# Four layer-norms on GpSimd, two constants first on VectorE, the last stores on two DMA queues, and a new list of pieces

## The chip, the cores and the metric

The kernel runs on one core of one Trainium2 chip. A core has a matrix engine (TensorE, PE in the profile; its weight loads are PEld), three engines that work on rows of 128 partitions (VectorE, DVE; ScalarE, ACT; GpSimd, POOL) and SyncE (SP), which does nothing but issue DMA transfers. Each engine has its own stream of instructions and goes through it in order; semaphores tie the streams together. The metric is the time of one execution on the device, in microseconds (us); lower is better.

## The reference

One activation `x` of 2,048 tokens by 512 is normalized once and goes through two branches whose results are added to it: an attention with a memory that is carried over four segments of 512 tokens (32 heads of 16), and a dense layer with SiLU (512 to 1,792 to 512). All tensors are bf16.

```
xn = _layernorm(x, axis=-1)
return x + _A_ref(xn, A_wq, A_wk, A_wv, A_wo, A_beta) + _B_ref(xn, B_w1, B_w2)

# _A_ref, for each segment s of 4, L = 512
logits = jnp.einsum('bhqd,bhkd->bhqk', qs, ks) * scale + mask
p = _softmax(logits, axis=-1)
a_dot = jnp.einsum('bhqk,bhkd->bhqd', p, vs)
pq = phi(qs)
num = jnp.einsum('bhld,bhde->bhle', pq, M)
den = jnp.einsum('bhld,bhd->bhl', pq, z)[..., None] + 1e-06
o = g * (num / den) + (1.0 - g) * a_dot
pk = phi(ks)
M = M + jnp.einsum('bhld,bhle->bhde', pk, vs)
z = z + jnp.einsum('bhld->bhd', pk)
# after the segments: o @ wo

# _B_ref
out = jnp.einsum('bsf,fd->bsd', _silu(jnp.einsum('bsd,df->bsf', x, w1)), w2)
```

`phi(t)` is `t + 1` where `t > 0` and `exp(t)` elsewhere, `g` is the sigmoid of `A_beta` for each head.

## The kernel before

The tokens are 16 tiles of 128 (`x` tile `t`), four to a segment. For each segment `s` the kernel makes `k`, `q` (features on partitions, four blocks `dt` of 128 features, 8 heads each), `v` (tokens on partitions), the dense layer's hidden values `h` (14 blocks), the attention, and the output product, which adds 14 products of the dense layer and 4 of the attention into one bank of PSUM per tile.

The softmax of a segment and a `dt` is cut into five blocks, `S` number `20 s + 5 dt + b`. A block's scores fill `psS`, four banks of PSUM, of which there is one; one ScalarE instruction of 128 x 2,048 exponentiates them into a buffer `Pb` (seven of them), and GpSimd zeroes the upper triangle in the diagonal blocks (`scores`, L653 to L682; one mask instruction, or two where `b` is 1 or 4). Heads of odd number read `kTo`, a copy of `kT` with the even heads zeroed, which GpSimd makes behind each copy of `k` (L362). When the five blocks of a `dt` are there, `E` multiplies the weights with `v` for the even heads (blocks 0, 1, 2) and `O` for the odd ones (blocks 3, 1, 4); `V` carries ones beside the values, so each product brings its sums too. The copies out of PSUM (`Ev`, `Ov` on VectorE, `Ea`, `Oa` on ScalarE) are followed by moves on the SP queue: two that gather the sums into `zraw` (L711), and behind an odd copy four more that put the odd heads' rows into `oraw` (L730).

A segment's sums become reciprocals (`r`, or `R` for the last segment, where they come in two parts: the first three `dt`, then the fourth), are multiplied by the gate (`w`, `W`) and spread over partitions by two SP moves each (`z` for the attention's weights, `d` for the memory's; L542). Then `dv` scales the features, `n` multiplies them with the memory on TensorE, `zv` scales the attention's output, and `nv` adds the two into `oT`. The last output products of a tile read `oT` (pieces `o s.j.14` to `o s.j.17`, one for each `dt`; pieces `oc` and `od` are a half and a quarter of one, `oh` is half of the last tile's width, `st` and `sh` add `x` and store).

Nothing in the source's order of functions sets the order of work. A text, `ORDER` (L16), names every piece of work once, and the kernel issues the pieces in that order (L786 on); so the text fixes each engine's stream, and each queue's. The first letters say what a piece is and on which engine it runs: `k0.2.1` is a part of the product for `k` of segment 0, block 2; `kv` and `ka` are its copy on VectorE and ScalarE; `ha` is the tanh of the dense layer on ScalarE and `hv` its product on VectorE; `xs` are a tile's statistics on VectorE, `xg4.4` the inverse roots of tiles 4 to 7 on GpSimd, `Nv` a norm on VectorE and `Na` on GpSimd, `XD` the transpose of a normalized tile by DMA (SP); `fp`, `fa`, `fv` and `gp`, `ga`, `gv` are the parts of phi of `k` and `q` on GpSimd, ScalarE and VectorE; `t`, `m`, `mv` the memory's product; `xl` loads a tile of `x` again for the final sum; `lw` loads weights. Each line of `ORDER` after the first begins with an `S`, so a line is what is issued between two blocks of scores.

Between blocks of scores TensorE works on four groups of columns of 32 (lines L324, L696 of the profile, form 128*32) or on the whole array (L322); scores work on groups of rows (L662).

Before the list, outside it, the loads of `x` and the weights are issued, `zraw` is zeroed on VectorE, `ident` and `b16` are made on GpSimd. `make_odd` reads `b16` and makes `pm_odd`, which `kTo` needs; `make_kind` reads `ident` and makes four small vectors that the sums of segment 0 are the first to need.

Of the kernel before, what the change touches and what calls it, by code (L numbers as in the profile page):

```python
# [16 lines left out]
ones0 ones1 zeros xc0 xd0 xc1 xq0 xi0 Nv0 busy44 xd1 xq1 xc2 xi1 X0.1 Nv1 xd2 Xa0.1 busy6 v0.0.0 v0.0.1 xq2 X1.1 Xa1.1 xs3 v0.0.2 v0.0.3 xq3 v0.1.0 xi2 v0.1.1 v0.1.2 v0.1.3 odd Nv2 xi3 X2.1 va0.0 k0.2.0 va0.1 Nv3 Xv2.1 X3.1 Xv3.1 k0.0.0 k0.0.1 k0.0.2 k0.0.3 q0.0.0 kv0.0 tb q0.0.1 q0.0.2 xs4 q0.0.3 qa0.0 k0.2.1 q0.3.0 fa0.0 q0.1.0  # L17
S1 k0.2.2 xs6 q0.1.1 v0.3.0 v0.3.1 xs7 q0.3.1 q0.1.2 q0.1.3 xs5 xg4.4 q0.3.2 qa0.1 q0.3.3 fp0.0
S2 k0.2.3 v0.3.2 qv0.3 v0.3.3 k0.1.0 kv0.2 fp0.2 fa0.2 k0.1.1 vv0.3 k0.1.2 k0.1.3 q0.2.0 q0.2.1
S3 kv0.1 q0.2.2 h0.10.0 h0.10.1 Nv4 fv0.0 q0.2.3 h0.10.2 v0.2.0 h0.10.3 qv0.2 ha0.10 k0.3.0 k0.3.1  # L20
S0 Nv5 v0.2.1 k0.3.2 hv0.10 h0.11.0 k0.3.3 h0.11.1 h0.11.2 kv0.3 h0.11.3 Nv7 xs8 XD5 ha0.11 h0.7.0
S7 h0.7.1 h0.1.0 h0.7.2 h0.7.3 v0.2.2 h0.1.1 v0.2.3 XD4 h0.1.2 h0.1.3 hv0.11 Nv6 ha0.7
S6 h0.13.0 fp0.3 XD7 h0.13.1 vv0.2 hv0.7 E0 XD6 v1.1.0 h0.13.2 h0.13.3 ha0.1 v1.1.1 Ev0
S5 fv0.2 h0.5.0 v1.1.2 h0.5.1 hv0.1 v1.1.3 vv1.1 v1.3.0 h0.5.2 ha0.13 xs14 hv0.13 h0.5.3 ha0.5 t0.2 v1.3.1
S9 hv0.5 xs12 q1.1.0 v1.3.2 v1.3.3 fa0.3 q1.1.1 q1.1.2 E1 k1.1.0 q1.1.3
S4 qv1.1 k1.1.1 vv1.3 fv0.3 k1.0.0 k1.0.1 k1.0.2 lw0 h0.4.0 k1.1.2 Ev1 h0.4.1 k1.0.3 k1.1.3 kv1.1
S17 h0.8.0 h0.8.1 kv1.0 h0.4.2 O0 xs10 h0.4.3 h0.2.0 Ov0 ha0.4
S10 h0.2.1 k1.2.0 xs11 xs9 k1.2.1 h0.2.2 k1.2.2 h0.2.3 h0.8.2 ha0.2 t0.3 hv0.4 xg8.4 t0.0 k1.2.3
# [73 lines left out]
def kernel(  # L102
# [19 lines left out]
    NT = S // P  # L122
# [11 lines left out]
    out_flat = out.flatten_outer_dims()  # L134
# [40 lines left out]
    def load_w(eng, w_sb, W, k0, k1):  # L175
# [11 lines left out]
        out=beta_r[:], in_=bass.AP(tensor=A_beta.tensor, offset=A_beta.offset, ap=[[1, H], [0, 4], [1, 1]])  # L187
# [646 lines left out]
```

## Time and profile before

| what | value |
|---|---|
| median of 3 runs | 229.09 us (228.93 to 229.31) |
| the profiled execution, time | 229.25 us |
| its span | 227.4 us |
| granted TensorE clock | 1.00 |
| 80 exponentials (L669), busy on ScalarE | 150.2 us, 1.878 each |
| 56 tanh (L457), busy on ScalarE | 32.8 us |
| first and 80th exponential, start | 12.89 and 205.93 us |
| HBM | 9.96 MB read, 2.10 MB written, 53 GB/s over the span |

The profile is of one execution, with times from the start of its span. Busy time counts what an engine executes; "idle before" is the time an engine sat still ahead of an instruction, and behind the arrow stands what ended it. In a timeline a row is a run of like instructions, with start and length in us; an engine's name with a q is its sequencer (SPq issues DMAs). In busy time by stretch a row has the stretch, its length, the busy time and the number of instructions of PE, PEld, DVE, ACT and POOL, then the granted clock, the busy share of the DMA engines and GB/s.

### The profile page before, as it was taken

Reading aid. Unit: us, or ns where it says so; the run is one execution under the profiler, and the core shown is the slowest. Engines: PE = TensorE matmul, PEld = TensorE weight load, DVE = VectorE, ACT = ScalarE, POOL = GpSimd, SP = SyncE. Lnnn points to the kernel's source line nnn. Section 1 sums busy time; section 2 is a strip of 40 time slices with the busy share of each in tenths; the row PEclk is TensorE's granted clock in tenths of the full one; section 3 lists DMA queues with packets and bytes.
Section 4 is the critical chain, followed back from the end, with each engine's and each line's share of the span. In section 5 each row is a group of like instructions: output and inputs, shape, how many; then the busy total and the mean of one; then the engine's idle time right before and its main releaser. Section 6 shows DMA issues by size and latency. Waiting matters only on the chain.

```text
span 227.4 us, 7551 instructions
## 1 busy us (share of the span) xinstructions
PE 217.5 (96%) x3127; PEld 113.3 (50%) x3155; DVE 177.1 (78%) x350; ACT 198.5 (87%) x180; POOL 113.9 (50%) x173
## 2 busy tenths in 40 slices
PE   8999999999999999999999999999999999999993
PEld 8676645545444434444544444445444544445661
DVE  3799899987897797658798898846776987985834
ACT  3799998999999999999999899999999989897000
POOL 6049647767454673665544578545464364342000
PEclk9999999999999999999999999999999999999999
DMA  6991419323215213414123312141132212024032
GB/s 189 369 379 46 85 36 313 62 45 66 61 22 156 73 35 48 95 34 100 36 61 87 90 45 59 32 119 40 37 93 65 80 40 81 31 68 128 16 95 95
DMA packets 34787, 20.55 MB, mean 90 GB/s; under 512 B 15680, under 2 KB 34240, under 8 KB 34752
## 3 DMA queue, kind: packets, MB, share of 16 engines
q1 hardware_dynamic: 32128, 17.45, 28.0%
q10 hardware_dynamic: 2624, 2.62, 3.6%
q8 instruction: 24, 0.39, 0.7%
q14 instruction: 11, 0.09, 0.1%
HBM read 9.96 MB, written 2.10 MB: 53 GB/s over the span
## 4 chain that ended last, share of the span: by engine, by line
PE 67%; ACT 17%; DVE 7%; issue 4%; POOL 2%; DMA 1%; DVEq 0%; SPq 0%; ACTq 0%
PE ps L322 20%; PE psO L322 13%; ACT Pb L669 12%; PE psO L324 8%; PE psS L662 8%; PE ps L324 6%; PE psV L696 5%; PE psS L324 3%; ACT th L457 3%; PE psS L756 2%; ACT ex L395 1%; DVE hT L462 1%; DVE kT L361 1%; DVE qT L371 1%; DVE xn_t L301 1%
## 5 line engine op out<-in xcount | busy, mean ns | idle before, releaser
L669 ACT ACTIVATE Pb<-psS 128x2048 bf16<-128x2048 f32 x80 | 150.2, 1878 | 4.7 <-PE psS L662 4.0
L677 POOL TENSOR_SCALAR_AFFINE_SELECT Pb<-Pb 128x512 bf16<-128x512 bf16 (+1 forms) x112 | 79.1, 720 | 84.3 <-ACT Pb L669 83.0
L462 DVE SCALAR_TENSOR_TENSOR hT<-th,ps 128x512 bf16<-128x512 bf16 x56 | 37.7, 679 | 14.4 <-ACT th L457 13.7
L322 PE MATMUL ps<-xnT,w_sb 128*128 128x512 bf16 (+1 forms) x177 | 43.3, 340 | 0.8 <-issue 0.5
L322 PE MATMUL psO<-w_sb,hT 128*128 128x512 bf16 (+2 forms) x137 | 36.0, 339 | 0.7 <-issue 0.5
L457 ACT ACTIVATE th<-ps 128x512 bf16<-128x512 f32 x56 | 32.8, 598 | 0.6 <-PE ps L322 0.6
L324 PE MATMUL psO<-w_sb,hT 128*32 128x512 bf16 (+2 forms) x476 | 27.6, 301 | 0.0
L322 PEld LDWEIGHTS <-w_sb 128*128 128x128 bf16 x184 | 17.1, 98 | 16.3 <-issue 3.3
L696 PE MATMUL psV<-Pb,Vz 128*32 128x128 bf16 (+3 forms) x512 | 23.1, 300 | 0.2
L324 PE MATMUL ps<-xnT,w_sb 128*32 128x512 bf16 (+1 forms) x384 | 21.8, 329 | 0.0
L322 PEld LDWEIGHTS <-hT 128*128 128x128 bf16 x147 | 13.4, 98 | 16.6 <-issue 4.8
L324 PEld LDWEIGHTS <-hT 128*32 128x32 bf16 x644 | 15.9, 97 | 9.3 <-issue 1.7
L662 PE MATMUL psS<-qT,kT 16*128 16x128 bf16 (+3 forms) x256 | 17.3, 301 | 0.9 <-ACT Pb L669 0.8
L696 PEld LDWEIGHTS <-Vz 128*32 128x32 bf16 x512 | 13.1, 96 | 10.3 <-DVE hT L462 1.1
L662 PE MATMUL psS<-qT,kTo 32*128 32x384 bf16 (+3 forms) x256 | 17.2, 299 | 0.6 <-ACT Pb L669 0.2
L362 POOL TENSOR_SCALAR kTo<-kT,pm_odd 128x512 bf16<-128x512 bf16 x16 | 12.3, 771 | 8.4 <-DVE kT L361 7.5
L322 PE MATMUL ps<-xnT,wk_sb 128*128 128x512 bf16 (+1 forms) x66 | 15.4, 328 | 0.7 <-issue 0.5
L322 PE MATMUL ps<-wv_sb,xnT 128*128 128x512 bf16 x48 | 14.3, 380 | 0.6 <-DVE odd L726 0.2
L662 PEld LDWEIGHTS <-kT 16*128 16x128 bf16 x256 | 5.9, 91 | 16.7 <-issue 16.2
L361 DVE CAST kT<-ps 128x512 bf16<-128x512 f32 x15 | 10.2, 689 | 4.9 <-PE ps L322 4.3
L322 PE MATMUL ps<-xnT,wq_sb 128*128 128x256 bf16 (+1 forms) x62 | 12.8, 324 | 0.4 <-issue 0.2
L726 DVE CAST odd<-psV 128x512 bf16<-128x512 f32 x15 | 10.3, 687 | 3.5 <-PE psV L696 3.4
(106 smaller groups left out, 295.4 us busy)
## 6 DMA issues: line engine op xcount, KB each, us to landing
spr<-rz SPq DMA_DIRECT2D x56, 64.0 KB
x_res<-in_A_x_dram SPq DMA_DIRECT2D x16, 128.0 KB
out_dram<-o_out SPq DMA_DIRECT2D x15, 128.0 KB
w_sb<-in_B_w_dram SPq DMA_DIRECT2D x1, 1792.0 KB
w_sb<-in_B_w_dram ACTq DMA_DIRECT2D x1, 1792.0 KB
x_hi<-in_A_x_dram SPq DMA_DIRECT2D x2, 512.0 KB
oraw<-odd SPq DMA_DIRECT2D x64, 16.0 KB
wv_sb<-in_A_wv_dram SPq DMA_DIRECT2D x2, 256.0 KB
```

The source lines that it names most:

```text
L322: return [nc.tensor.matmul(out, lhsT=lhsT, rhs=rhs, start=start, stop=stop, skip_group_check=True)]
L324: nc.tensor.matmul(out[c : c + 32], lhsT=lhsT[:, c : c + 32], rhs=rhs, start=start, stop=stop, tile_position=(0, c), skip_group_check=True,)
L361: copy(out=kT[:, dt, :], in_=sts[s].pop(("k", dt))[:, :])
L362: nc.gpsimd.tensor_scalar(out=kTo[:, dt, :], in0=kT[:, dt, :], scalar1=pm_odd[:, 0:1], scalar2=1.0, op0=ALU.mult, op1=ALU.mult,)
L457: nc.scalar.activation(out=th[:], in_=sts[s]["h", ft][:, :], func=AF.Tanh, scale=0.5)
L462: nc.vector.scalar_tensor_tensor(out=st["hT"][:, ft, :], in0=st.pop(("th", ft))[:], scalar=1.0, in1=st.pop(("h", ft))[:, :], op0=ALU.add, ...
L662: nc.tensor.matmul(psS[:, g, c0 : c0 + nq], lhsT=kk[rows, dt, kt * P : (kt + 1) * P], rhs=st["qT"][rows, dt, kt * P : L], start=True, stop ...
L669: exp = nc.scalar.activation(out=Pb[:, :, :], in_=psS[:, :, :], func=AF.Exp, scale=SCALE)
L677: mask = nc.gpsimd.affine_select(out=blocks, in_=blocks, compare_op=ALU.is_ge, fill=0.0, base=0, pattern=[[0, blocks.shape[1]], [1, P]], c ...
L696: nc.tensor.matmul(psV[32 * g : 32 * g + 32, kt * P : L], lhsT=Vzs[s % 2][:, kt, 4 * dt + g, par : par + 2, :].rearrange("p a d -> p (a d) ...
L726: copy(out=odd[:], in_=sts[s].pop(("psV", 1))[:, :])
L756: nc.tensor.matmul(idle[:, 0:P], lhsT=zraw[:, 0:P], rhs=zraw[:, 0:P], start=True, stop=True)
```

## The change

The list of pieces is a new one over the same pieces, but for eight: `Nv7`, `Nv8`, `Nv9`, `Nv14` become `Na7`, `Na8`, `Na9`, `Na14` (the norms of four tiles on GpSimd), `kv0.0` becomes `ka0.0`, `vv0.3` becomes `va0.3`, `Ev9` becomes `Ea9` (copies that go from VectorE to ScalarE), and `qa0.1` becomes `qv0.1` (one that goes the other way). `kind` and `odd` stand first in the list; they stood in the line of `S22` and among the first norms. The order of nearly all other pieces differs in some places. In the code, the stores of the last segment's tiles 0 and 2 and of the first half of tile 3 are issued by ScalarE's queue, where SP issued all.

From the list, the head, the lines that the prediction speaks of and the end (lines of `ORDER` are whole):

```diff
@@ ORDER @@
-ones0 ones1 zeros xc0 xd0 xc1 xq0 xi0 Nv0 busy44 xd1 xq1 xc2 xi1 X0.1 Nv1 xd2 Xa0.1 busy6 v0.0.0 v0.0.1 xq2 X1.1 Xa1.1 xs3 v0.0.2 v0.0.3 xq3 v0.1.0 xi2 v0.1.1 v0.1.2 v0.1.3 odd Nv2 xi3 X2.1 va0.0 k0.2.0 va0.1 Nv3 Xv2.1 X3.1 Xv3.1 k0.0.0 k0.0.1 k0.0.2 k0.0.3 q0.0.0 kv0.0 tb q0.0.1 q0.0.2 xs4 q0.0.3 qa0.0 k0.2.1 q0.3.0 fa0.0 q0.1.0
...
-S74 o2.3.16 h3.12.0 st2.3 h3.12.1 ha3.12 h3.2.0 gv3.1 E14
-S73 h3.2.1 ha3.2 Ev14 oc2.2.5.1 o2.1.2 o2.2.16 o2.1.6 hv3.12 h3.8.0 o2.2.10 st2.2 hv3.2 o2.1.1 o2.1.5 h3.8.1 ha3.8 hv3.8
-S79 o2.1.0 O14 Ov14 od2.1.12.2 s3 sv3 r3.1 o2.1.7 r3.3 h3.7.0 r3.2 r3.0 oc2.1.10.0 od2.1.12.3 o2.1.3 w3
-S77 h3.6.0 R0.0 oc2.1.11.0 h3.7.1 R0.1 ha3.7 h3.6.1 hv3.7 d3.2 o2.1.14 R0.3 h3.9.0 ha3.6 hv3.6 o2.1.15
-S76 o2.1.8 d3.0 d3.1 h3.9.1 o2.1.9 oc2.1.10.1 h3.13.0 ha3.9 od2.1.12.0 oc2.1.11.1 h3.13.1 xl3.3 hv3.9 o3.0.12 o2.1.16 ha3.13 o2.1.13
-S75 o3.0.5 hv3.13 o2.1.4 o3.0.4 R0.2 W0 o2.1.17 z3.0 h3.10.0 o3.1.8 h3.10.1 dv3.0 z3.2 ha3.10 od2.1.12.1 st2.1 o3.0.0 o3.1.6
-S78 o3.0.9 hv3.10 dv3.1 o3.1.1 h3.11.0 o3.0.8 h3.11.1 dv3.2 E15 oh13.1 oh4.1 ha3.11 z3.1 o3.2.13 Ea15 oh12.1 hv3.11 oh6.1 oh10.1 o3.2.1 O15 Oa15 oh11.1 oh2.1 oh12.0 o3.0.1 zv3.0 oh13.0 n3.1 od3.1.11.3 oh3.1 zv3.1 o3.2.0 oh10.0 n3.0 o3.1.2 nv3.0 o3.0.7 nv3.1 o3.1.12 oh9.1 oh8.0 o3.2.5 oh11.0 o3.1.7 o3.2.6 o3.0.13 oh8.1 R1.1 R1.0 o3.2.9 o3.1.14 d3.3 R1.3 o3.2.14 oc3.0.3.0 oh0.0 o3.0.6 o3.2.8 oc3.0.11.1 zv3.2 o3.1.10 n3.2 o3.2.10 oh9.0 R1.2 oh1.1 oh15.0 W1 nv3.2 oh15.1 o3.2.4 oc3.0.11.0 o3.1.5 o3.0.14 o3.2.11 oh1.0 o3.2.12 o3.2.2 oh6.0 o3.2.16 oh2.0 z3.3 oh7.0 oh0.1 dv3.3 oh3.0 od3.0.10.0 oh14.0 od3.1.11.1 oc3.1.0.0 o3.0.15 zv3.3 od3.1.11.0 oc3.0.3.1 n3.3 oc3.1.9.0 oh4.0 o3.2.3 xl3.0 o3.1.16 nv3.3 o3.2.15 od3.0.10.1 od3.0.10.2 o3.2.7 oh5.0 oh16.0 oh16.1 od3.0.10.3 oh14.1 o3.2.17 oh17.0 oh17.1 o3.0.2 o3.0.16 o3.0.17 od3.1.11.2 xl3.1 st3.2 oc3.1.9.1 oh7.1 oh5.1 sh0 o3.1.17 sh1 oc3.1.0.1 o3.1.3 o3.1.15 o3.1.13 st3.0 o3.1.4 st3.1
+kind odd ones0 ones1 zeros xc0 xd0 xc1 xq0 xi0 Nv0 busy44 xd1 xq1 xc2 xi1 X0.1 Nv1 xd2 Xa0.1 busy6 v0.0.0 v0.0.1 xq2 X1.1 Xa1.1 xs3 v0.0.2 v0.0.3 xq3 xi2 va0.0 v0.1.0 v0.1.1 v0.1.2 Nv2 v0.1.3 X2.1 va0.1 xi3 k0.0.0 Nv3 Xv2.1 X3.1 tb Xv3.1 k0.0.1 k0.2.0 k0.0.2 k0.0.3 xs4 q0.0.0 ka0.0 q0.0.1 q0.0.2 q0.0.3 k0.2.1 qa0.0 fa0.0 v0.3.0 k0.1.0
+S0 v0.3.1 q0.1.0 xs6 v0.3.2 xs7 xs5 xg4.4 k0.1.1 k0.2.2 q0.1.1 v0.3.3 va0.3 q0.1.2 Na7
+S2 k0.1.2 k0.2.3 XD7 k0.3.0 k0.1.3 kv0.2 fa0.2 k0.3.1 q0.1.3 k0.3.2 q0.3.0 kv0.1 k0.3.3 kv0.3 qv0.1
+S3 Nv5 h0.10.0 h0.10.1 Nv4 q0.3.1 fp0.2 h0.10.2 h0.11.0 h0.10.3 h0.11.1 h0.11.2 ha0.10 XD4 hv0.10 q0.3.2
...
+S12 hv0.2 h0.6.0 vv1.2 h0.6.1 h0.6.2 t0.0 k1.3.2 Na9 q1.0.0 fa0.1 h0.6.3 hv0.8 O1
+S17 k1.3.3 xs15 q1.0.1 Nv10 Ov1 Nv11 q1.0.2 kv1.3 Na8 h1.11.0 ha0.6 q1.0.3 qv1.0 h1.11.1 fv0.1 h1.11.2
...
+S28 od0.0.11.1 o0.2.1 Ev4 Na14 fa1.2 od0.2.0.0 od0.2.0.2 q2.3.0 q2.3.1 oc0.2.9.0 o0.2.4 o0.2.8 XD14 qv2.3 oc0.0.13.0 t1.1
...
+S49 vv3.2 k3.2.0 hv2.8 k3.2.1 kv3.2 fv2.1 E9 d1.0 Ea9 O8
...
+S73 Ev14 h3.8.0 h3.8.1 o2.1.9 gv3.0 o2.1.15 h3.2.0 ha3.8 hv3.12 h3.2.1 gv3.1 hv3.8 ha3.2 o2.1.16
+S75 O14 hv3.2 od2.1.12.2 oc2.1.10.1 Ov14 h3.6.0 h3.6.1 s3 ha3.6 sv3 o2.1.1
+S78 h3.7.0 h3.13.0 o2.1.13 hv3.6 r3.3 r3.1 r3.0 r3.2 h3.13.1 ha3.13 xl2.1 hv3.13 od2.1.12.3 w3 h3.9.0 h3.9.1 ha3.9 h3.7.1 ha3.7 o2.1.3
+S77 o2.1.7 o3.0.5 o2.1.4 o2.1.5 hv3.9 R0.1 od2.1.12.0 h3.10.0 h3.10.1 hv3.7 R0.2 h3.11.0 ha3.10 R0.0
+S76 R0.3 o2.1.17 o2.1.8 d3.1 o3.0.9 d3.0 od2.1.12.1 h3.11.1 o3.0.6 hv3.10 o3.1.13 o3.0.8 W0 ha3.11 o3.1.1 oc2.1.11.1 oc2.1.11.0
+S79 d3.2 o3.0.13 o3.1.10 dv3.1 hv3.11 o3.1.5 o3.0.0 z3.0 E15 o2.1.2 od3.0.10.3 o2.1.6 o2.1.14 oc2.1.10.0 oh4.1 oh7.1 dv3.2 z3.1 oh6.1 o3.2.6 oh6.0 z3.2 o3.2.1 o3.2.10 Ea15 oc3.0.11.1 O15 st2.1 zv3.1 o3.1.12 n3.1 o3.1.8 dv3.0 o3.2.8 oh11.0 Oa15 o3.2.13 d3.3 zv3.0 oh5.0 oh12.1 n3.0 nv3.1 o3.2.3 o3.2.15 o3.2.12 zv3.2 oc3.1.0.1 oh1.0 n3.2 nv3.0 oh0.1 o3.1.2 od3.0.10.0 nv3.2 o3.0.14 o3.2.2 o3.2.5 oh3.1 R1.2 o3.2.9 o3.1.7 R1.1 R1.0 o3.0.12 oh7.0 oh0.0 oh8.0 o3.0.15 oc3.1.0.0 o3.1.3 oh14.1 o3.0.2 R1.3 oc3.0.3.0 oh16.0 W1 dv3.3 oh11.1 oh2.0 oh16.1 o3.2.14 z3.3 oc3.1.9.0 oh14.0 oh15.1 o3.2.7 o3.0.4 oh3.0 od3.1.11.3 oh10.0 o3.1.6 o3.2.0 oc3.1.9.1 oh2.1 oh9.0 xl3.0 oh13.0 oc3.0.11.0 xl3.3 zv3.3 n3.3 oh13.1 od3.0.10.1 o3.0.1 o3.2.11 o3.0.7 o3.2.16 oh9.1 nv3.3 oc3.0.3.1 o3.2.4 oh15.0 oh10.1 o3.2.17 oh1.1 o3.0.16 od3.0.10.2 od3.1.11.2 od3.1.11.0 oh8.1 o3.0.17 od3.1.11.1 oh12.0 oh17.1 o3.1.16 o3.1.4 st3.2 st3.0 oh5.1 o3.1.15 oh17.0 oh4.0 sh1 sh0 o3.1.14 o3.1.17 st3.1
@@ -588,7 +588,8 @@
         )
         if s == LAST and j >= 2:
             fin_out.append(((j,), out))
-        nc.sync.dma_start(out=out_flat[t * P : (t + 1) * P, :], in_=o_out[:])
+        queue = nc.scalar if s == LAST and j % 2 == 0 else nc.sync
+        queue.dma_start(out=out_flat[t * P : (t + 1) * P, :], in_=o_out[:])
 
     def out_mm(s, j, i, half=None, part=0, parts=1):
 
@@ -634,7 +635,8 @@
             out=o_half[:], in0=st["psO", j, h], scalar=0.5, in1=st["x", j][:, cols], op0=ALU.mult, op1=ALU.add
         )
         fin_out.append(((j, h), out))
-        nc.sync.dma_start(out=out_flat[(NT - 1) * P : NT * P, cols], in_=o_half[:])
+        queue = nc.sync if h else nc.scalar
+        queue.dma_start(out=out_flat[(NT - 1) * P : NT * P, cols], in_=o_half[:])
 
     def out_store(s, j):
         assert len(sts[s].pop(("done", j))) == 4 * (FT + DT)
```

More of the change, by code (lines that the diff above doesn't have):

```diff
@@ new lines @@
+S36 st0.1 od0.3.10.1 o0.3.17 E6 Ev6 o0.3.4 h1.12.0 h1.12.1 h1.12.2 h1.12.3 ha1.6
+S35 fv2.0 o0.3.3 hv1.6 v2.3.0 v2.3.1 h1.13.0 h1.13.1 mw0.0 vv2.3 ha1.12 hv1.12 h1.13.2 h1.13.3 t1.3 gp1.3
+S37 o0.3.6 q2.0.0 gp1.2 q2.0.1 od0.3.10.2 O6 ha1.13 qv2.0 Ov6 o0.3.16 hv1.13
+S39 k3.1.0 k3.1.1 ga1.3 E7 q3.3.0 xl1.2
+S38 o0.3.9 Ev7 oc0.3.13.0 q3.3.1 h1.2.0 gv1.3 gv1.2 ga2.2 h1.2.1 o0.3.12 oc0.3.11.0 h1.2.2 o0.3.7
+S40 kv3.1 m1.2 qv3.3 o0.3.2 O7 h1.2.3 o0.3.15 mv1.2 ha1.2 o0.3.14
+S43 Ov7 o0.3.5 q3.0.0 q3.0.1 q3.1.0 q3.1.1 hv1.2
```

133 lines of the change are left out of this document (60 added, 73 removed).

## The prediction

> **What bounds the kernel now.** I read the page first (busy shares, costliest groups), then busy time by stretch, then the order of time around one softmax block, then the end.
>
> ```profile
> PE 217.5 (96%) x3127; PEld 113.3 (50%) x3155; DVE 177.1 (78%) x350; ACT 198.5 (87%) x180; POOL 113.9 (50%) x173
> L669 ACT ACTIVATE Pb<-psS 128x2048 bf16<-128x2048 f32 x80 | 150.2, 1878 | 4.7 <-PE psS L662 4.0
> ```
>
> ```profile
> 40.00:60.00 20.00, 19.34 (x336) 10.71 (x338) 17.42 (x36) 19.94 (x18) 13.57 (x22) 1.00 0.32 63
> 140.00:160.00 20.00, 19.79 (x311) 9.46 (x310) 13.24 (x24) 19.88 (x18) 11.02 (x15) 1.00 0.22 56
> 210.00:220.00 10.00, 10.00 (x264) 6.59 (x256) 5.96 (x12) 0.43 (x1) 0.00 (x0) 1.00 0.22 59
> ```
>
> The reader sees two engines full at once: between 40 and 160 us TensorE and ScalarE are both busy for over 19 of 20 us, VectorE and GpSimd are not. After 210 us only TensorE is full. The order of time in the middle shows why:
>
> ```profile
> 99.71 1.88 ACT L669 ACTIVATE Pb<-psS 128x2048 bf16<-128x2048 f32 x1
> 101.48 0.59 ACT L457 ACTIVATE th<-ps 128x512 bf16<-128x512 f32 x1
> 102.09 1.88 ACT L669 ACTIVATE Pb<-psS 128x2048 bf16<-128x2048 f32 x1
> ```
>
> One exponential (piece S) and one small ScalarE operation make a beat of 2.38 us. There is one psS, so the next scores are written while the small operation runs. From the start of the first exponential (12.89) to that of the 80th (205.93) are 193.04 us, 79 beats. I class them by what lies between two S in the list: a beat with no or one small operation takes 2.37 to 2.40, one with two 2.73, and where TensorE has more than 5,120 columns to stream (a 512-column group takes 0.217 us, a beat has 0.215 of changes of array shape) it takes columns x 0.424 ns + 0.215. That gives 59 x 2.38 + 4 x 2.73 + 16 TensorE-bound beats of 41.54 together = 192.9 to 193.2 by rounding, against 193.04 measured: the list runs almost without a stall. One that is there:
>
> ```profile
> 22.40 0.10 PEld L662 LDWEIGHTS <-kTo 32*128 32x128 bf16 x4 [0.28 <-POOL kTo L362]
> 22.75 1.88 ACT L669 ACTIVATE Pb<-psS 128x2048 bf16<-128x2048 f32 x1 [0.30 <-PE psS L662]
> ```
>
> The end, after the last exponential, is TensorE work (17.1 us of columns) beside one chain: O15 (209.07), its copy on ScalarE, six moves on the SP queue, reciprocals, four more moves, two VectorE products, and only then the last output products of that quarter:
>
> ```profile
> 197.54 2.44 SPq L730 DMA_DIRECT2D oraw<-odd  x4
> ...
> 211.64 3.54 SPq L730 DMA_DIRECT2D oraw<-odd  x4
> 215.23 2.73 SPq L542 DMA_DIRECT2D spr<-rz  x4
> ```
>
> ```profile
> 219.50 0.43 DVE L554 TENSOR_TENSOR oT<-spr,oraw 128x512 bf16<-128x512 bf16 x1 [0.87 <-DMA spr<-rz]
> 220.03 0.69 DVE L573 TENSOR_TENSOR oT<-ps,oT 128x512 bf16<-128x512 f32 x1
> 220.78 0.34 PEld L324 LDWEIGHTS <-oT 128*32 128x32 bf16 x12 [0.24 <-DVE oT L573]
> ...
> 223.15 1.28 DVE L586 SCALAR_TENSOR_TENSOR o_out<-psO,x_res 128x512 bf16<-128x512 f32 x2
> ...
> 224.18 0.81 SPq L591 DMA_DIRECT2D out_dram<-o_out  x2
> ```
>
> TensorE waits 0.24 us for that chain, so the chain and TensorE end the kernel together. SP issues without a pause from 196.35 to 218.93.
>
> **The change, part by part.** Counted over both lists: columns are the same (464,640), changes of array shape too (160), so TensorE has no less to do. The exact differences are eight copies or norms that change engine, the place of kind and odd, and the order.
>
> *Constants first.* kind is five VectorE instructions (0.21, 0.15, 0.14, 0.16, 0.15, from its rows at 62.4 us), odd one of 0.14 (at 7.59): 0.95 us. VectorE is idle for 2.51 us before the first statistics at 3.56, and GpSimd has made ident by 1.35 and b by 1.92, so they fit before 3.56: cost 0. Without that cover 0.95 would go in front of the norms. Where they leave gains nothing: odd stood ahead of Nv2, but the fourth norm waits for ScalarE's root at 8.19, and VectorE is not what TensorE waits for at 62 us.
>
> *Copies that change engine.* k0.0, v0.3 and the even copy of 9 go to ScalarE (0.59 each), q0.1 comes back. VectorE loses 2 x 0.69 net, ScalarE gains 1.2. ka0.0 runs at 11.25, when the exp table is loaded, and q0.0's copy needs TensorE until 11.8 anyway: the first exponential stays at 12.9 (+-0.1). va0.3 takes the place of qa0.1 in the first beat; Ea9 goes into a beat that would have held no small operation.
>
> *Four norms on GpSimd.* The rows:
>
> ```profile
> L301 DVE TENSOR_SCALAR xn_t<-x_hi,mv_all,rstd_all x8: 399/409/846, 17.5 to 49.0; 128x512 bf16<-128x512 bf16 x8
> L362 POOL TENSOR_SCALAR kTo<-kT,pm_odd x16: 686/692/1014, 11.7 to 165.7; 128x512 bf16<-128x512 bf16 x16
> ```
>
> (Tile views, ns: least, median, most.) VectorE is spared 4 x 0.41 to 0.85 = 1.6 to 3.4 us. GpSimd has no norm in the trace; the nearest row is the same operation on the same shape, kTo: 4 x 0.69 to 1.01 = 2.8 to 4.1 us, of 114 busy; I take 0.7 each. Behind a norm on GpSimd stand masks and kTo, and TensorE waits for these. Na7 stands in the first beat; behind it and the root are the mask of the next beat and three kTo. I add from the mask of the first block at 14.8: 0.64 + 1.21 (roots) + 0.7 + 1.14 + 3 x 0.7 gives 20.6 or, by 1.01 for each kTo, 21.5; the first of them is needed by the fifth exponential at 22.0: cost 0, and if 1.5 us more came in front, each further microsecond counts. For the other three the tiles are needed 7 beats or more later. What VectorE's relief buys is the stall above at most: -0.28. It is at the most half a microsecond since TensorE waits for VectorE in few other places.
>
> The Trainium skill (SBUF — State Buffer, "The single rule") speaks against this part: VectorE and GpSimd share a port pair that one instruction holds to its end, and VectorE takes part in a 2-port mode or with two SBUF inputs. The trace fits: the same norm takes 0.41 us alone and 0.85 beside a GpSimd pos at 20.22. By that rule each moved norm may hold up a VectorE instruction by some 0.7 us and give back most of what it spared; then the -0.28 falls away and the sum below would be 0.28 higher.
>
> *The order.* The same classes over the new list: 59 beats of 2.38, 4 of 2.73 and 16 TensorE-bound ones of 41.72 (S78, with three small operations and 7,808 columns, 3.52 alone): +0.15 against the old list.
>
> *The end of the list.* The last S is now S79, which has two masks (0.58 apart) where S78 had one. Call the last scores T. The masks are done at T+3.75, TensorE comes to O15 at T+3.97 (3.64 of columns and 0.33 as before): no wait, but O15 is 0.38 later after T than before (T+3.59). Everything on the chain follows on SP in the same order (two, four, two, two moves), so the last oT is ready 0.38 later. TensorE arrives earlier by 0.16 of columns and simply waits, 2.7 us of columns stand behind it in both lists: +0.38. Bounds: 0 if some of the chain is faster, +0.4.
>
> *Two queues.* st3.2, st3.0 and the first half go to ScalarE's queue, idle since 210.43, so nothing waits behind them. In the old list the last o_out on VectorE began 0.13 us after TensorE's end, behind the one for j=0, which is now earlier in the list: -0.13. The last store was issued at 224.62, 0.19 after its data, behind another store's issue of 0.34; alone 0.07: -0.12. The transfer after it (some 2.0 us to its landing) stays. Bounds for both: 0 (the landing hides them) and -0.5 (a quarter of the landing saved as well).
>
> The Trainium skill (DMA: Bandwidth & Descriptors, "Issuing engines are not separate DMA queues") says that SP and ScalarE share the DMA engines, so that a second queue saves issue time alone; by that the -0.12 is all there is, and the bound of -0.5, for which a landing would have to get shorter, is out of reach. The trace of before has no stores on two queues to test it.
>
> Sum against the profiled execution of 229.25 (span 227.4 and 1.85 around it, 0.16 above the median): 0 + 0 - 0.28 + 0.15 + 0.38 - 0.13 - 0.12 = 0.00. On the median's scale 229.1.
>
> **Rivals.** *Faster, by the move that stalls.* The fourth oraw move of O15 took 1.10 us longer than its like (3.54 against 2.44 for four) and stands in the chain. For: such long issues come at five places only (66, 99, 115, 188, 213 us), and a new order moves them. Against: the number of moves before it is nearly the same. If it lies elsewhere, the chain loses its 0.38 and the 0.24 of idle TensorE too: 229.09 + 0.15 - 0.28 - 0.25 - 0.24 = 228.5.
>
> *Slower, by the SP queue before O15.* z3.0, z3.1, z3.2 now stand right in front of the moves of E15 and O15; z3.2 needs a spr buffer that the product dv3.2 frees. It decides from where z3.2 starts later than T+2.3 (its two moves 1.3, E15's 1.2, a store 0.5, O15's copy done at T+5.4). I place it at T+1.3. For it: SP had no pause there, w3 comes a beat later in the list; against: the margin of 1 us. Price one pair of moves: 229.1 + 1.3 = 230.4.
>
> *Slower, on GpSimd.* If the norms' real time is nearer to 1.5 us than to 0.7, or they come between an exponential's end and its mask when E or O is next, TensorE waits. For: beats two to four hold some 8 us of GpSimd work in 7.1. Against: 50% busy over the span, and only one wait for it before. Two such waits of 0.7: 230.5.
>
> *The change does nothing it says*, as both ends are hidden: that is the forecast itself.
>
> **How the numbers follow.** Forecast 0.31, faster 0.29, SP 0.26, GpSimd 0.14. Predicted 229.1; its own range 228.6 to 229.6. 0.2% is 0.46 us, about what can be told from no change, so faster 0.29, same 0.31, slower 0.40. The range takes in the rivals and one more stall: 228.1 to 231.0.
>
> **What would show it.** First exponential at 12.9 and the 80th 192.9 us later; kind and odd over before 3.6; the wait for kTo at the fifth exponential gone; norms on GpSimd of 0.7; O15 at T+4.0 and a TensorE wait for oT of some 0.7 us; the last store issued within 0.1 of its data. A longer wait of SP before O15's moves, masks later than 0.2 us after their exponential, or several beats over 2.45 in the first 60 would prove it wrong.

## The result and the profile after

The median after is 231.25 us (230.91 to 231.44, 4 runs), beside 229.19 for the kernel before on the same chip: a ratio of 1.0090 with a 95% interval of 1.0072 to 1.0107. That is 2.06 us slower, and outside the range predicted. The profiled execution took 230.91 us (span 229.0, granted clock 0.997); against the 229.25 and 227.4 of before it is 1.66 longer, and 1.6 in the span.

Where the time lies is read from three points of the span:

| stretch | before, us | after, us | difference |
|---|---|---|---|
| start of the span to the first exponential | 12.89 | 12.63 | -0.26 |
| first to 80th exponential (starts) | 193.04 | 194.91 | +1.87 |
| 80th exponential to the end of the span | 21.51 | 21.46 | -0.05 |

The first row is scatter: over all runs of this study it lies between 12.45 and 13.04, for equal heads too. So the loss is in the 79 beats. The page of after has GpSimd 10.0 us busier (113.9 before), VectorE 3.8 less busy and, in the row of the exponentials, 0.6 us more idle time:

```profile
PE 220.3 (96%) x3116; PEld 113.4 (50%) x3116; DVE 173.3 (76%) x344; ACT 199.5 (87%) x182; POOL 123.9 (54%) x177
...
L671 ACT ACTIVATE Pb<-psS 128x2048 bf16<-128x2048 f32 x80 | 150.3, 1879 | 5.3 <-PE psS L664 4.2
```

Busy time by stretch of after (columns as before) shows two stretches hurt. From 40 to 60 us before had ScalarE (the fourth busy time of a row) 19.94 busy, TensorE (the first) 19.34 and GpSimd (the fifth) 13.57; from 140 to 160 it had ScalarE 19.88 busy:

```profile
40.00:60.00 20.00, 18.45 (x366) 10.54 (x364) 16.26 (x31) 19.24 (x19) 17.30 (x22) 1.00 0.31 61
140.00:160.00 20.00, 19.69 (x290) 9.19 (x292) 11.22 (x23) 19.38 (x17) 10.32 (x14) 1.00 0.25 62
```

Beat by beat, against the prediction's classes, these beats of after are too long: S15 by 0.76 (3.49 us where the class has 2.73), S55 by 0.51 (2.89), S29 by 0.36 (2.74), S75 by 0.23, S42 0.16, S78 0.15, S40 0.12, S46 0.11, S16 0.09: 2.49 in all, while four TensorE-bound ones came out 0.75 shorter than their class. S40, S46 and S78 are as long in the run below that mends all three parts and is level with before, so their excess is an error of the classes and no wait. The one stall of before, 0.28 at S0, is gone.

The tile view of the normalized tiles gives what a norm costs on GpSimd (ns: least, median, most):

```profile
L301 POOL TENSOR_SCALAR xn_t<-x_hi,mv_all,rstd_all x3: 2067/2067/2072, 16.7 to 49.7; 128x512 bf16<-128x512 bf16 x3
L301 POOL TENSOR_SCALAR xn_t<-x_end,mv_all,rstd_all x1: 2495/2495/2495, 78.3 to 78.3; 128x512 bf16<-128x512 bf16 x1
```

Three times the 0.7 us that the prediction took, and above its upper bound of 1.01. The order of time on GpSimd around the longest beat (start, length):

```profile
45.75 2.07 POOL L301 TENSOR_SCALAR xn_t<-x_hi,mv_all,rstd_all 128x512 bf16<-128x512 bf16 x1
47.79 1.09 POOL L679 TENSOR_SCALAR_AFFINE_SELECT Pb<-Pb 128x1024 bf16<-128x1024 bf16 x1
48.98 0.69 POOL L362 TENSOR_SCALAR kTo<-kT,pm_odd 128x512 bf16<-128x512 bf16 x1
49.66 2.07 POOL L301 TENSOR_SCALAR xn_t<-x_hi,mv_all,rstd_all 128x512 bf16<-128x512 bf16 x1
```

The next mask starts 2.04 us after the first norm does, so the lengths hold. The second norm (`Na8`) ends at 51.73. On VectorE, the product `hv1.11` begins there:

```profile
51.76 0.69 DVE L462 SCALAR_TENSOR_TENSOR hT<-th,ps 128x512 bf16<-128x512 bf16 x1 [0.76 <-POOL xn_t L301]
```

It does not read tile 8. Its buffer for `hT` is the one that held `x_hi`, which the norm reads, so it may write only when the norm has ended. By the kernel's source the norm reads block 4 of that buffer and the product writes block 11, so what is waited for is the release of the whole buffer and not the same data. Behind it the wait is handed on, from VectorE to TensorE (a bank of PSUM that the product frees) and from TensorE to the next tanh and exponential on ScalarE:

```profile
52.50 1.05 PE L324 MATMUL ps<-xnT,w_sb 128*32 128x256 bf16 x28 [0.59 <-DVE hT L462]
```

```profile
51.08 1.88 ACT L671 ACTIVATE Pb<-psS 128x2048 bf16<-128x2048 f32 x1
...
53.60 1.08 ACT L457 ACTIVATE th<-ps 128x512 bf16<-128x512 f32 x2 [0.64 <-PE ps L324]
54.57 1.89 ACT L671 ACTIVATE Pb<-psS 128x2048 bf16<-128x2048 f32 x1
```

S55, with no norm near, is of another kind. A mask of GpSimd took 1.63 us where the like take 1.09 to 1.14, beside a VectorE product with two SBUF inputs, and `E10` stands right behind it on TensorE. GpSimd, VectorE and TensorE of after around 143 us:

```profile
143.10 1.63 POOL L679 TENSOR_SCALAR_AFFINE_SELECT Pb<-Pb 128x1024 bf16<-128x1024 bf16 x1 [1.80 <-ACT Pb L671]
```

```profile
143.09 0.68 DVE L405 SCALAR_TENSOR_TENSOR pk<-ex,pos 128x512 bf16<-128x512 bf16 x1
```

```profile
144.78 0.29 PE L698 MATMUL psV<-Pb,Vz 128*32 128x256 bf16 x4 [0.31 <-POOL Pb L679]
```

S29 is the same met from the other side: two VectorE products of segment 0 (0.42 each alone) took 1.52 together beside `kTo` and `pos` on GpSimd, and TensorE waited 0.27 for `oT`. The Trainium skill (SBUF — State Buffer, "Who interferes with whom", the single rule) says that these two engines share a pair of ports that one instruction holds to its end; the trace agrees, by 1.63 against 1.09 and 1.52 against 0.84. That the ports are the cause of these two lengths rests on that rule and on these durations; no run separates it from other causes.

The end, VectorE and SP of after (the twelve `spr` moves stand ahead of those of `E15`):

```profile
223.46 0.69 DVE L586 SCALAR_TENSOR_TENSOR o_out<-psS,x_res 128x512 bf16<-128x512 f32 x1 [1.60 <-PE psS L324]
224.07 0.68 DVE L586 SCALAR_TENSOR_TENSOR o_out<-psO,x_res 128x512 bf16<-128x512 f32 x1
224.67 0.74 DVE L634 SCALAR_TENSOR_TENSOR o_half<-psS,x_res 128x256 bf16<-128x256 f32 x2
225.33 0.68 DVE L586 SCALAR_TENSOR_TENSOR o_out<-psO,x_res 128x512 bf16<-128x512 f32 x1
```

```profile
202.10 8.81 SPq L542 DMA_DIRECT2D spr<-rz  x12
...
213.86 2.46 SPq L732 DMA_DIRECT2D oraw<-odd  x4
216.36 2.73 SPq L542 DMA_DIRECT2D spr<-rz  x4
...
226.04 0.34 SPq L592 DMA_DIRECT2D out_dram<-o_out  x1
```

The move that took 1.10 us too long before is not there (2.46 for four, 3.54 before). But one of the twelve spreads, issued at 204.17, took 1.33 us where the others took about 0.60. So the moves of `E15` began 0.7 and those of `O15` 0.46 later after the 80th exponential than in four runs below in which this list has no such issue (four norms back, stores early, norm as a product, four moves), and TensorE waited 0.29 for the last `oT`. TensorE ends at 224.82, 17.28 after the 80th exponential, where it was 17.69; in those four it is 17.08. But `st3.2` now stands behind `oh17.1`, could not begin before 223.46, and the last five operations of VectorE run in a row until 226.01, 1.19 behind TensorE. That is 18.47 after the 80th exponential, against 18.50 before: what the chain gained was lost again behind TensorE, in the stores.

### The profile page after: what moved, and what is told of

It is laid out like the page before. It is cut to its first block, busy times and chain, and to the rows that moved or that the text cites. A ratio compares the mean times of both kernels' runs of the same rounds, so it can differ in the third digit from the quotient of the medians.

```text
span 229.0 us, 7519 instructions
## 1 busy us (share of the span) xinstructions
PE 220.3 (96%) x3116; PEld 113.4 (50%) x3116; DVE 173.3 (76%) x344; ACT 199.5 (87%) x182; POOL 123.9 (54%) x177
## 4 chain that ended last, share of the span: by engine, by line
PE 62%; ACT 17%; DVE 7%; POOL 6%; issue 4%; SPq 2%; DMA 1%; DVEq 0%; POOLq 0%
PE ps L322 17%; ACT Pb L671 12%; PE psO L322 10%; PE psO L324 8%; PE ps L324 7%; PE psS L664 7%; PE psV L698 5%; PE psS L324 3%; POOL Pb L679 3%; ACT th L457 2%; PE psS L758 2%; POOL xn_t L301 2%; ACT ex L395 2%; POOL kTo L362 1%; DVE hT L462 1%
## 5 line engine op out<-in xcount | busy, mean ns | idle before, releaser
L679 POOL TENSOR_SCALAR_AFFINE_SELECT Pb<-Pb 128x512 bf16<-128x512 bf16 (+1 forms) x112 | 81.7, 745 | 76.3 <-ACT Pb L671 75.4
L322 PE MATMUL ps<-xnT,w_sb 128*128 128x512 bf16 (+1 forms) x211 | 50.7, 342 | 0.1
L322 PEld LDWEIGHTS <-w_sb 128*128 128x128 bf16 x211 | 19.5, 98 | 18.2 <-issue 3.5
L698 PE MATMUL psV<-Pb,Vz 128*32 128x384 bf16 (+3 forms) x512 | 23.1, 300 | 0.5 <-POOL Pb L679 0.5
L664 PE MATMUL psS<-qT,kT 16*128 16x256 bf16 (+3 forms) x256 | 17.3, 301 | 0.7 <-ACT Pb L671 0.4
L664 PE MATMUL psS<-qT,kTo 32*128 32x256 bf16 (+3 forms) x256 | 17.2, 299 | 0.6 <-ACT Pb L671 0.6
L324 PE MATMUL ps<-xnT,w_sb 128*32 128x256 bf16 (+1 forms) x276 | 14.9, 322 | 0.6 <-DVE hT L462 0.6
L371 DVE CAST qT<-ps 128x512 bf16<-128x512 f32 x15 | 10.2, 684 | 5.3 <-PE ps L322 4.5
L322 PE MATMUL ps<-xnT,wk_sb 128*128 128x256 bf16 (+1 forms) x62 | 14.1, 325 | 0.1
L586 DVE SCALAR_TENSOR_TENSOR o_out<-psO,x_res 128x512 bf16<-128x512 f32 x14 | 9.6, 687 | 6.0 <-PE psO L324 3.2
```

Of the source, the lines that this page charges most:

```text
L322: return [nc.tensor.matmul(out, lhsT=lhsT, rhs=rhs, start=start, stop=stop, skip_group_check=True)]
L324: nc.tensor.matmul(out[c : c + 32], lhsT=lhsT[:, c : c + 32], rhs=rhs, start=start, stop=stop, tile_position=(0, c), skip_group_check=True,)
L371: copy(out=seg_tile(s, "qT")[:, dt, :], in_=sts[s].pop(("q", dt))[:, :])
L586: out = nc.vector.scalar_tensor_tensor(out=o_out[:], in0=st.pop(("psO", j)), scalar=0.5, in1=st["x", j][:], op0=ALU.mult, op1=ALU.add)
L664: nc.tensor.matmul(psS[:, g, c0 : c0 + nq], lhsT=kk[rows, dt, kt * P : (kt + 1) * P], rhs=st["qT"][rows, dt, kt * P : L], start=True, stop ...
L679: mask = nc.gpsimd.affine_select(out=blocks, in_=blocks, compare_op=ALU.is_ge, fill=0.0, base=0, pattern=[[0, blocks.shape[1]], [1, P]], c ...
```

## Theories, and the experiments

Theory A: the loss is the length of a GpSimd norm, and what waits behind it in that engine's stream. Rival B: it is the new list, in places that have nothing to do with the norms (S29, S55, S75 and the stores). Rival C: the norm is long for its form (two per-partition values, or the subtraction) rather than for the engine. Further, what two queues and the early constants are worth by themselves. Runs of one group share a chip and its runs of the kernel before; medians of before were 228.72 (first four runs), 229.03 (the next four) and 229.18 (the last four), so ratios are compared. After stands at 1.0090. In diffs of the list a piece has a line of its own.

### The norms back on VectorE, in the new list

```diff
-Na7
+Nv7
...
-Na9
+Nv9
...
-Na8
+Nv8
...
-Na14
+Nv14
```

> The changed list, the four norms back on VectorE in the same places. Theory (a norm on GpSimd costs 2.1 us, not 0.7, and only the one of tile 8 is on the path, through hv1.11; the rest of the loss is the new order): the beat S15 falls from 3.49 to 2.73 us, the others stay, 231.25 - 0.8 = 230.4 us. Rival A (the norms are the whole loss): 229.2 or less. Rival B (GpSimd's norms are hidden and the order is all): 231.2 or a little more, since VectorE gets 1.6 to 3.4 us back.

Measured: 233.48 us, ratio 1.0199 (1.0172 to 1.0227). No theory had that. S15 went back to its class, but S2, S13 and S29 grew to 3.67, 3.73 and 3.67 (class 2.38 each). At two of them the norm needs the inverse roots that GpSimd makes right before it; on GpSimd it simply followed them, on VectorE it holds up all that stands behind:

```profile
16.45 0.42 DVE L301 TENSOR_SCALAR xn_t<-x_hi,mv_all,rstd_all 128x512 bf16<-128x512 bf16 x1 [1.87 <-POOL rstd_all L286]
...
77.56 0.41 DVE L301 TENSOR_SCALAR xn_t<-x_end,mv_all,rstd_all 128x512 bf16<-128x512 bf16 x1 [2.22 <-POOL rstd_all L286]
```

At S13 two norms beside masks took 1.21 and 0.85, and TensorE waited 1.00 for a copy of `q`. So list and engines belong together; this run doesn't give the price of the norms.

### One norm back

```diff
-Na8
+Nv8
```

> The changed list, only the norm of tile 8 back on VectorE. Theory: the same as with all four back, 230.4 us, with S15 at 2.73. Rival A (each of the four costs its part): 230.8 to 231.0. Rival B (the norms are hidden): 231.2.

Measured: 230.71, ratio 1.0069 (1.0046 to 1.0092). S15's 0.76 is gone, as A has it, and S18, three beats later, is 0.94 too long: TensorE waits for the transpose of tiles 8 to 11.

```profile
59.77 0.59 PE L322 MATMUL ps<-xnT,wk_sb 128*128 128x512 bf16 x2 [0.88 <-DMA xnT<-xn_t]
```

`XD8` is issued on SP at 54.67, behind the moves of `Ev2`, so the transpose lands late whichever engine makes the norm. In after, the stall at S15 had covered this one.

### The four norms on GpSimd, in the old list

```diff
-Nv7
+Na7
...
-Nv9
+Na9
...
-Nv8
+Na8
...
-Nv14
+Na14
```

> The old list, nothing changed but the norms of tiles 7, 8, 9 and 14 on GpSimd in VectorE's places. Theory: in the old list the norm of tile 8 stands right in front of hv1.11 and behind the mask of S14, which ends some 2.5 us after its exponential begins; 2.1 us of norm behind that make hv1.11 some 2 to 3 us late: 231.2 to 232.2 us, the wait in the beats S14 or S15. Rival (0.7 us a norm, hidden): 229.2 to 229.6.

Measured: 235.91, ratio 1.0299 (1.0270 to 1.0328): the right place, and several times the price. S14 took 7.87 us, 5.49 over its class, and S15 4.07, where its class has 2.38. GpSimd and VectorE of this run:

```profile
51.67 1.23 POOL L677 TENSOR_SCALAR_AFFINE_SELECT Pb<-Pb 128x512 bf16<-128x512 bf16 x2 [0.28 <-ACT Pb L669]
52.89 2.07 POOL L301 TENSOR_SCALAR xn_t<-x_hi,mv_all,rstd_all 128x512 bf16<-128x512 bf16 x1
```

```profile
54.99 0.69 DVE L462 SCALAR_TENSOR_TENSOR hT<-th,ps 128x512 bf16<-128x512 bf16 x1 [5.51 <-POOL xn_t L301]
```

It is the same `hv1.11` and the same buffer. The norm is 2.07 long, but it also stands behind masks of blocks that come late, and the product waits for all of it.

### Other forms of the norm

```diff
+        mean, root, op0, op1 = mv_all[:, t, 0:1], rstd_all[:, t, 0:1], ALU.subtract, ALU.mult
+        if t == 7:
+            root = 1.0
+        if t == 9:
+            op0 = ALU.mult
+        if t == 14:
+            op0, op1 = ALU.mult, ALU.add
```

> The changed list with other arithmetic in three of GpSimd's norms (the output is then not the normalized one): tile 7 subtracts the mean and multiplies by the constant 1, tile 8 is as it was, tile 9 multiplies by both vectors, tile 14 multiplies by one and adds the other. Theory (two operands that are a vector over partitions cost the time): tile 7 takes 0.7 us like kTo, the three others 2.1. Rival (the subtraction costs it): tiles 7 and 8 take 2.1, tiles 9 and 14 take 0.7. Rival (the tile that is read, x_hi or x_end, or the bf16 source from DMA): all four 2.1.

Three of the four tiles are then not normalized; the run serves for the lengths alone. Its tile view (one execution, 230.91 us):

```profile
L308 POOL TENSOR_SCALAR xn_t<-x_hi,mv_all,rstd_all x2: 761/1418/2076, 46.0 to 49.1; 128x512 bf16<-128x512 bf16 x2
L308 POOL TENSOR_SCALAR xn_t<-x_hi,mv_all x1: 2003/2003/2003, 16.8 to 16.8; 128x512 bf16<-128x512 bf16 x1
L308 POOL TENSOR_SCALAR xn_t<-x_end,mv_all,rstd_all x1: 1186/1186/1186, 78.8 to 78.8; 128x512 bf16<-128x512 bf16 x1
```

Tile 7, subtract and one vector: 2.00 us. Tile 8, the norm as it was: 2.08. Tile 9, multiply and multiply, two vectors: 0.76. Tile 14, multiply and add: 1.19, at a place where other work ran. The number of vectors does not matter (two cost 0.76 and 2.08); what the slow ones share is the subtraction first.

The same execution shows more. S15 is in its class (2.73), though the norm of tile 8 still takes 2.08: as the norm of tile 9 ahead of it is short, it ends 0.24 before the exponential of S15 begins, where in after it ended 0.64 behind that. So the wait at S15 came of both norms in GpSimd's stream, and not of one alone. S18 is then 1.07 too long, for the same late transpose as with one norm back.

### The norm as a product

So `(x - mean) * root` becomes `x * root + (-mean * root)`, the second term a 128x1 operation ahead of it:

```diff
+        if eng is nc.gpsimd:
+            eng.tensor_scalar(
+                out=shift[:, t : t + 1], in0=mv_all[:, t, 0:1], scalar1=rstd_all[:, t, 0:1], scalar2=-1.0,
+                op0=ALU.mult, op1=ALU.mult,
+            )
+            eng.tensor_scalar(
+                out=xn[t][:], in0=xs(t, t + 1)[:, 0, :], scalar1=rstd_all[:, t, 0:1], scalar2=shift[:, t : t + 1],
+                op0=ALU.mult, op1=ALU.add,
+            )
+            return
```

> The changed list; GpSimd's norm is x * root + (-mean * root), with one small instruction for the second vector: the same values without the subtraction. Theory (the subtraction costs 1.3 of its 2.07 us, and the late norm of tile 8 holds hv1.11 and TensorE): 0.8 to 1.2 us a norm, S15 falls from 3.49 to 2.8, and as the last transpose of tiles 8 to 11 still stands behind the moves of Ev2 on SP, S18 may take some of it back, as it took 0.94 with one norm back on VectorE: 0.2 to 0.8 us less than the change. Rival (the waits of the new list are all the loss, the norms' length nothing): no difference. Rival (the length of the norms is the whole loss): 2 us less, level with before.

```profile
L307 POOL TENSOR_SCALAR xn_t<-x_hi,rstd_all,shift x3: 762/762/762, 17.3 to 49.8; 128x512 bf16<-128x512 bf16 x3
L307 POOL TENSOR_SCALAR xn_t<-x_end,rstd_all,shift x1: 762/762/762, 78.8 to 78.8; 128x512 bf16<-128x512 bf16 x1
```

All four take 0.762 us. The time is 230.50, ratio 1.0059 (1.0038 to 1.0081): 0.0031, or 0.7 us, less than after (the two intervals overlap from 1.0072 to 1.0081, so the size is loose; the beat agrees, with 0.76 gone at S15 and 0.42 come at S18, and the rest not told apart). S15 is in its class; S18 has 0.42 of the late transpose. S29, S55 and S75 stay as they were. So A holds for about a third of the loss, and B has to carry the rest.

### The last stores earlier

```diff
 o3.2.17
+st3.2
 oh1.1
...
 o3.0.17
+st3.0
 od3.1.11.1
...
 o3.1.4
-st3.2
-st3.0
 oh5.1
```

> The changed list, with st3.2 right behind o3.2.17 and st3.0 right behind o3.0.17. Theory (st3.2 stands behind oh17.1 in the list and waits for it, since both write the tile of psS; then five VectorE operations stand in a row and end 1.2 us after TensorE): st3.2 begins at once, VectorE's last begins when TensorE ends, the tail from the start of the 80th exponential to the end of the span falls from 21.5 to 21.0, 0.5 us less than the change. Rival (TensorE's end or the landing decides): no difference over 0.1 us.

Measured: 230.51, ratio 1.0061 (1.0042 to 1.0080), 0.66 us less than after. `st3.2` began at 222.58 and VectorE ended 18.06 after the 80th exponential, 0.42 earlier than in after. But about half of that is the long issue of SP in after: five runs with the stores where after has them (four norms back, one back, the other forms, the norm as a product, four moves) have 18.28 as well. From the 80th exponential to the end of the span it is 21.12 us here, and 21.02 to 21.25 in those five. So the profile shows the store begin earlier and the span not end earlier; the size of this part rests on the medians alone, whose intervals overlap (1.0072 to 1.0080).

### Four pieces moved

```diff
@@ S14, S16 @@
 XD9
+XD8
...
 mv0.2
-XD8
@@ S29 @@
 O4
-zv0.2
 oc0.0.4.1
 zv0.1
+zv0.2
@@ S55 @@
 fv2.2
-E10
 o1.0.17
 oc1.1.4.0
 oc1.1.9.0
 o1.2.17
+E10
@@ S75 @@
-O14
 hv3.2
 od2.1.12.2
 oc2.1.10.1
+O14
```

> The changed list with only the four pieces moved (XD8 in front of Ev2's moves, zv0.1 in front of zv0.2, E10 behind three output products, O14 behind two); the norms subtract as in the change, the stores stand where they stood. Theory (two separate causes): S29, S55 and S75 fall to 2.4 to 2.5 us, S15 stays at 3.4 to 3.5; 0.7 to 1.0 us less than the change, 0.4 to 0.6% above before. Rival (the long norms make these three beats late too, by shifting GpSimd): less than 0.4 us less than the change.

Measured: 230.12, ratio 1.0027 (0.9997 to 1.0056), 1.4 us less than after by the ratios. The excesses of S29 and S55 are gone and S75's fell from 0.23 to 0.07, 1.03 us together; S15 is still 3.49. The one profiled execution (230.56) shows no shorter distance (195.32), since other beats came in it: S70 by 0.83, S42 0.40, S26 and S39 0.26 each. At S70 a spread by DMA, issued by 182.15, released VectorE only at 185.63; in after the same product ran at 184.91:

```profile
185.63 0.85 DVE L564 TENSOR_TENSOR phiQT<-spr,phiQT 128x512 bf16<-128x512 bf16 x1 [1.03 <-DMA spr<-rz]
```

S42 and S70 are in their class in the profile of the next kernel, which has the same four moves. So this is the landing of a transfer in one execution, and the size of the gain rests on the median and on the beats that went.

### All three together

The norm as a product, the stores earlier and the four moves, as in the diffs above.

> The changed list with the norm as a product, the stores early, and four pieces moved: XD8 in front of Ev2's moves, zv0.1 in front of zv0.2, E10 behind three output products, O14 behind two. Theory (the new order sets an operation where it needs something that GpSimd or VectorE, slowed by each other, has not finished): S15 2.8, S18 2.4, S29 2.4, S55 2.4, S75 2.45, tail 21.0; 2.0 to 2.4 us less than the change, level with before or 0.3 below it. Rival (each wait that goes comes back at the next tight place): 0.5 to 1.2 us less than the change.

Measured: 228.80, ratio 0.9989 (0.9971 to 1.0007): level with before, 2.3 us better than after. First to 80th exponential is 193.12 us, where before has 193.04; S15, S18, S29 and S55 are in their class, S75 is 0.06 over. The end did not fall to the 21.0 us expected: it took 21.99 in the profiled execution (229.53, 0.7 above the median), where a spread landed late and TensorE waited 1.20 us for the product behind it. The three parts one by one sum to 2.8; the difference to 2.3 is within their intervals.

### Two queues and the constants, in the old list

The diff of the stores is that of the change; the constants are `kind` and `odd` first in the list. Three runs: both, the queues only, the constants only.

> The old list, with the last stores on two queues and kind and odd first on VectorE, nothing else. Theory (both are hidden but for the wait of the last store for the issue before it): kind and odd are over by 2.3 us, the last store is issued 0.05 to 0.1 us after its data instead of 0.19, time 0 to 0.2 us less than before, not to be told from it. Rival (the two parts carry a gain of their own that the new list lost): 0.5 us or more less than before.

> The old list and nothing but the last stores on two queues. Theory: the last store is issued 0.1 us earlier after its data, 0.1 us less than before, not to be told from it. Rival (what the old list with both parts gained, 0.5 us, comes from the queues): 0.4 to 0.6 us less.

> The old list and nothing but kind and odd first on VectorE. Theory: hidden in the wait for the first tile, no difference. Rival (odd stood in the way of the second pair of norms): 0.2 to 0.5 us less than before, first exponential earlier by as much.

Measured: both 228.52, ratio 0.9980 (0.9958 to 1.0001); queues only 228.46, ratio 0.9963 (0.9940 to 0.9985); constants only 229.01, ratio 0.9992 (0.9966 to 1.0018). The constants do nothing, and the two queues alone beat both kernels. VectorE and SP of the queues' run:

```profile
223.31 1.28 DVE L586 SCALAR_TENSOR_TENSOR o_out<-psO,x_res 128x512 bf16<-128x512 f32 x2
```

```profile
211.78 3.56 SPq L732 DMA_DIRECT2D oraw<-odd  x4
...
224.62 0.34 SPq L592 DMA_DIRECT2D out_dram<-o_out  x1
```

The last store is issued 0.03 after its data (224.59), not 0.19. That is 0.16; the median gained 0.72 beside before on this chip (0.85 by the ratio) and the interval's lower end is 0.34. In the profile another 0.25 is in the landing: 2.57 us from the last issue to the end of the span (2.58 in the two other runs of the old list with two queues), against 2.82 before, 2.83 in the run with the constants only and 2.66 with the four norms alone, which have one queue. The rest is not in the profile. Part of it can be scatter: the fastest executions, 228.17 here and 228.39 before, are 0.22 apart, while the 35 of before reach up to 231.41 and the 12 of this run only to 228.98. Besides, the store ahead of the last one was issued 0.59 before it and not 0.44; whether that shortens the landing no run tests. The Trainium skill (DMA: Bandwidth & Descriptors, "Issuing engines are not separate DMA queues") has a second queue save issue time alone; this run gained more, and why is open. With the new list, where the stores come closer together, two queues had 2.71 to 3.03.

### The old list mended

Before, with the two queues and the constants, `kv0.1` earlier (the stall of S0) and the stores `st3.2` and `st3.0` earlier:

```diff
@@ S2, S3 @@
 k0.1.3
+kv0.1
 q0.2.0
...
-kv0.1
 q0.2.2
@@ S78 @@
 o3.2.17
+st3.2
 oh17.0
...
 o3.0.17
+st3.0
```

> The old list with both parts of the change that it can take, kv0.1 moved in front of the mask of S3, and st3.2 and st3.0 right behind their last products. Theory: the wait for kTo in the beat S0 goes (0.28), VectorE's last store begins when TensorE ends (0.1), two queues (0.1): 0.4 to 0.6 us less than before, under both kernels. Rival (such waits come back in the next beat): level with the old list that has both parts.

Measured: 229.30, ratio 1.0003 (0.9978 to 1.0029): nothing gained. S0's wait is gone, and S6 is 1.09 too long in the profiled execution. There, VectorE, GpSimd and TensorE:

```profile
23.95 1.32 DVE L301 TENSOR_SCALAR xn_t<-x_hi,mv_all,rstd_all 128x512 bf16<-128x512 bf16 x1
25.19 0.68 DVE L378 CAST Vz<-ps 128x512 bf16<-128x512 f32 x1
```

```profile
24.03 1.09 POOL L679 TENSOR_SCALAR_AFFINE_SELECT Pb<-Pb 128x1024 bf16<-128x1024 bf16 x1 [0.83 <-ACT Pb L671]
```

```profile
25.92 0.73 PE L698 MATMUL psV<-Pb,Vz 128*32 128x512 bf16 x16 [0.95 <-DVE Vz L378]
```

A norm met a mask, took 1.32 instead of 0.41, and the copy of `v` behind it came late.

## Why the prediction was wrong, point by point

*What bounds the kernel.* Right: two engines full, a beat of 2.38, and a loss or gain counts only where a beat grows or shrinks. The classes held too, within 0.3 where nothing waited.

*The norms: the term that was mis-sized.* The prediction took 0.7 us for a norm on GpSimd, by the row of `kTo`, "the same operation on the same shape". It measured 2.07 to 2.50. `kTo` is a multiplication; the run of forms shows that the subtraction makes the difference. The bounds from a near row were too narrow since the row differed in the one thing that mattered, the arithmetic.

*The step that failed with it.* "For the other three the tiles are needed 7 beats or more later." The waiter was not a reader of the tile but a writer to the buffer of its input. The prediction followed who needs what the norm makes and never asked who needs what it holds. The norm as a product shows the price of the two errors together: 0.7 us.

*The order: the larger failure.* "59 beats of 2.38 …: +0.15 against the old list" (its own terms, 41.72 less 41.54, give +0.18) sums work and leaves out the distance between an operation and what it needs on another engine. By these classes the new list's 79 beats take 193.06; they took 194.91. The four moves, which change no work at all, took 1.0 of it away by the beats S29, S55 and S75, and 1.4 by the medians. Its own sign of being wrong, several beats over 2.45 in the first 60, came: S15, S16, S29, S40, S42, S46 and S55.

*The rival "slower, on GpSimd"* had the right mechanism, at 0.14: real time "nearer to 1.5 us than to 0.7", a mask late ahead of `E`. Its 230.5 was within 0.8 of the result, yet for one wait of 0.76, and for S29 and S55, where VectorE and GpSimd worked beside each other.

*The rival "slower, by the SP queue before O15"* came in part. With T as the prediction has it, the start of the last scores (207.09 in after), `z3.2` started at T+2.58, behind the bound of T+2.3; the prediction had it at T+1.3, and in the four runs without a long issue it is T+1.86. It was not the wait for a `spr` buffer, as the queue had no pause there, but one issue of 1.33 us. It made the last `oT` 0.46 late, not 1.3.

*kTo's stall, -0.28:* gone, as forecast. *Constants, 0:* they ran at 1.38 to 2.17 us, hidden, and alone change nothing. *Copies, 0:* no beat shows them.

*O15 and the chain, +0.38:* it did not come. `O15` began at T+3.75, 0.16 later than before and not 0.38, and the long issue left the moves of `O15`, as in the faster rival: the last `oT` was ready 0.47 earlier after the 80th exponential, TensorE still waited 0.29 for it (0.7 forecast), and ended 0.41 earlier. *Two queues, -0.13 and -0.12:* the last issue stood 0.03 behind its data, as forecast, but "the one for j=0, which is now earlier in the list" overlooked that `st3.2` went behind `oh17.1`. So the end gained nothing in after, while in the old list the same queues gained more than both terms by the medians (at least 0.34 by the interval).

## What to carry to other kernels

Before an operation changes engine, look for a row with the same arithmetic there, not only the same shape, and if there is none, keep the range wide. Follow its buffers both ways: who waits for what it writes, and who may not write until it has read. A list tuned for one placement of work carries waits that show only when another goes away; so sum beats for the work, and then go through the tight ones for the operation that stands right behind its own releaser.

## What the runs showed of the hardware

A 128x512 bf16 tensor_scalar on GpSimd took 0.76 us as multiply-multiply or multiply-add, and 2.00 to 2.08 with a subtraction first (up to 2.57 beside other work); on VectorE the latter takes 0.41 alone, and 0.85 to 1.32 beside a mask of GpSimd.

Single issues of SP that take up to 1.1 us longer than their like come at changing places: on the fourth `oraw` move of `O15` in before and with the queues only (1.68 and 1.70, against 0.59 for the same move in after), on a spread ahead of `E15` in after (1.33 against 0.60). With the constants only, where the moves have the order of before, the four moves of `O15` took 2.45 and none was long, so the order alone does not set the place. What it waits for the traces don't show.

In the old list two queues for the last stores shortened the time by 0.34 us or more by the interval, where the issue that they save is 0.16; no run here tells why.
